# Which engine makes the rounded weight copies of the first MLP: ScalarE or GpSimd

## The chip, the core and the metric

The program runs on one core of a Trainium2 chip. The metric is the device time of one execution in microseconds. Four engines compute: TensorE (PE; its weight loads are shown as PEld), VectorE (DVE), ScalarE (ACT) and GpSimd (POOL). SyncE (SP) issues the DMA transfers.

## The reference

Windowed causal attention on 4 batches, 8 heads, 576 positions of dimension 64, and then two MLPs on the 2304 tokens of width 512, one behind the other:

```python
scores = scale * np.matmul(q, k.transpose(0, 1, 3, 2)) + slope[h] * -np.abs(rel)   # masked to 0 <= rel < 128
x = softmax(scores) @ v                                   # then tokens x 512
h = x @ w_in;   g = np.where(h >= 1, h, np.where(h <= -1, 0, (h + 1) ** 2 / 4));   x = g @ w_out     # 512 -> 2048 -> 512
h = x @ w_in2;  g = h * np.clip(h + 3.0, 0.0, 6.0) / 6.0;                          out = g @ w_out2
```

The MLP weights come as 64-bit floats.

## The kernel before

Matrix products run in a rounded 32-bit format (F32R). To keep accuracy every operand is held in two parts: a rounded copy, "hi", and the remainder, "lo" = x - hi. Each product is three matmuls (lo by hi, hi by lo, hi by hi). `split_hi(engine, hi, x)` writes the rounded copy and `split_lo` the remainder.

The weights of an MLP are converted on the chip, in 16 tiles f = 0 to 15 of 128 rows, each with 128 hidden columns of w_in and the matching 128 rows of w_out (2 x 512 numbers for each partition). SP loads the raw words into `raw`. `conv_tick` advances the conversion by one step: it issues the second and third part for tile f-1 and then the first part for tile f.

- `conv1`: ScalarE takes the magnitude of the high words (L194, into `m`); for the first MLP GpSimd makes the sign in place (L197, on every second word of `raw`); ScalarE rescales the low words (L198).
- `conv2`: VectorE shifts and joins (L205) and adds the low part (L212), both in `m`.
- `conv3`: the rounded copy of `m` goes to `hl[:, 0]` (the tile `w`, "wa" in the trace for the first MLP), on ScalarE (line L152, inside `split_hi`); VectorE makes the remainder (L159, inside `split_lo`).

`Weights("a", ..., True)` is the first MLP with `sign_pool` on; `Weights("b", ..., False)` the second MLP, which does without GpSimd.

The tokens of the first MLP go in blocks: three of 256 tokens, then four of 384. Attention for the first tokens runs alone with the first tiles' conversion; then blocks 0 and 1 take the hidden tiles 0 to 7, then both take tiles 8 to 15, while attention for later blocks is spread between (`run_block`, `spread`). For each tile f of a block TensorE does 12 matmuls into `h` (L659); VectorE, ScalarE and VectorE make the activation (L688, L689, L690), ScalarE copies its rounded part g (L152), GpSimd its remainder (L159); two tiles later (LAG = 2) 12 matmuls add it to `acc` (L701).

Attention in these stretches is: matmuls for scores (L411), row minimum on VectorE (L441), exponential on ScalarE (L445), transposes on TensorE (L469, L470), a copy to SBUF on ScalarE (L152, `tt`), matmuls with the values (L506), division on VectorE (L518 to L520), transpose (L531), and the split of x (ScalarE L152, VectorE L159).

SP's queue runs in the order written. On the other engines a planner of the framework orders the instructions up to the second MLP: it goes by the order in which the code traces them, and by when its own costs say that each is ready. Each engine then takes its instructions strictly in that order.

Of the kernel before, what the change touches and what calls it, by code (L numbers as in the profile page):

```python
# [40 lines left out]
def tile_window_attention_two_mlps(  # L41
# [108 lines left out]
    def split_hi(eng, hi, x):  # L150
        if eng == "act":
            nc.scalar.copy(hi, x)  # L152
        elif eng == "pool":
            nc.gpsimd.tensor_scalar(out=hi, in0=x, scalar1=1.0, scalar2=1.0, op0=ALU.mult, op1=ALU.mult)
        else:
            engines[eng].tensor_copy(hi, x)

    def split_lo(eng, lo, x, hi):
        engines[eng].tensor_tensor(out=lo, in0=x, in1=hi.bitcast(F32), op=ALU.subtract)  # L159
# [3 lines left out]
    class Weights:  # L163
# [50 lines left out]
        def conv3(self, f):  # L214
            del self.raw[f]
            m = self.m.pop(f)
            hl = wpool.tile([P, 2, 2, PIECE], F32R, tag=f"w{f}", name=f"w{self.nm}{f}")
            split_hi("act", hl[:, 0], m)
            split_lo("dve", hl[:, 1], m, hl[:, 0])
            self.hl[f] = hl  # L220

# [1119 lines left out]
```

## Time and profile before

| | |
|---|---|
| median of 3 runs | 948.38 us (946.82 to 948.67) |
| profiled execution | 947.39 us, span 945.7 us |
| TensorE busy | 929.6 us, 98% of the span |
| VectorE busy | 661.1 us, 70% |
| ScalarE busy | 534.0 us, 56% |
| GpSimd busy | 305.9 us, 32%, all of it before about 490 us |

TensorE's share is an average over stretches with different limits. What a change on another engine is worth has to be read from the stretch in which it acts: whether TensorE is idle there, and for whom it waits.

### The profile page before, as it was taken

The numbers are of one execution on the slowest core, as the hardware profiler recorded it, in microseconds if no ns is written. First come the engines' busy times: TensorE is split into PE (matmuls) and PEld (weight loads), VectorE is DVE, ScalarE is ACT, GpSimd is POOL, SyncE is SP. The second block draws the span as 40 slices with busy tenths as digits, with TensorE's granted clock in tenths as the row PEclk, the third lists the DMA queues.
The fourth block names the chain that finished last, engine by engine and source line by source line (L and its number), as shares of the span: only waits on it lengthen the run. The fifth ranks groups of instructions, "written<-read, shape, count | busy, mean of one in ns | idle before, by whom it ended". The sixth has DMA issues, their size and how long they took to land.

```text
span 945.7 us, 17240 instructions
## 1 busy us (share of the span) xinstructions
PE 929.6 (98%) x5683; PEld 875.8 (93%) x5683; DVE 661.1 (70%) x1750; ACT 534.0 (56%) x1349; POOL 305.9 (32%) x575
## 2 busy tenths in 40 slices
PE   8899999999999999999999999999999999999998
PEld 6799999999999999999999999999999898888987
DVE  5998975786677676767645999958557777644443
ACT  6998854676667566666634886535333334423233
POOL 3343854787668676767710000000000000000000
PEclk9999999999999999999999999999999999999999
DMA  9758332222212212222007861004264644544441
GB/s 263 233 168 262 112 99 88 68 81 72 73 54 82 72 52 62 80 84 56 7 34 249 304 235 59 1 23 167 79 211 166 236 170 147 170 124 114 122 113 67
DMA packets 95337, 114.90 MB, mean 122 GB/s; under 512 B 8848, under 2 KB 73616, under 8 KB 95248
## 3 DMA queue, kind: packets, MB, share of 16 engines
q1 hardware_dynamic: 95248, 113.80, 38.4%
q8 instruction: 45, 0.74, 0.3%
q14 instruction: 44, 0.36, 0.1%
HBM read 88.60 MB, written 25.17 MB: 120 GB/s over the span
## 4 chain that ended last, share of the span: by engine, by line
PE 86%; DVE 6%; DMA 3%; ACT 2%; issue 2%; POOL 0%; SPq 0%; ACTq 0%; POOLq 0%; DVEq 0%
PE h L659 25%; PE acc L760 21%; PE acc L701 17%; PE y L1242 7%; PE x L1242 5%; PE s L411 4%; PE r L554 3%; PE t L470 2%; PE r L506 1%; DMA rawa<-w_in 1%; DMA x2r<-x2d 1%; DVE r L688 1%; DMA kw<-kT 1%; DVE x L159 1%; DVE r L690 1%
## 5 line engine op out<-in xcount | busy, mean ns | idle before, releaser
L659 PE MATMUL h<-x,wa 128*128 128x384 f32 (+1 forms) x1344 | 231.0, 317 | 1.2 <-DVE r L690 0.8
L701 PE MATMUL acc<-g,wa 128*128 128x384 f32 (+1 forms) x1344 | 227.4, 315 | 0.4 <-POOL g L159 0.4
L760 PE MATMUL acc<-wb,g 128*128 128x512 f32 x861 | 222.2, 393 | 0.0
L659 PEld LDWEIGHTS h<-x,wa 128*128 128x128 f32 x1344 | 206.6, 189 | 4.4 <-DVE r L690 3.2
L701 PEld LDWEIGHTS acc<-g,wa 128*128 128x128 f32 x1344 | 206.2, 189 | 0.7 <-POOL g L159 0.6
L760 PEld LDWEIGHTS acc<-wb,g 128*128 128x128 f32 x861 | 159.4, 188 | 24.9
L152 ACT CAST g<-r 128x384 fp32r<-128x384 f32 (+1 forms) x208 | 101.3, 487 | 70.9 <-DVE r L1189 37.6
L159 POOL TENSOR_TENSOR g<-r,g 128x256 fp32r<-128x256 f32 (+1 forms) x96 | 92.9, 968 | 67.4 <-ACT g L152 54.3
L689 ACT ACTIVATE r<-r 128x384 f32<-128x384 f32 (+1 forms) x112 | 53.3, 478 | 82.9 <-DVE r L688 82.6
L159 DVE TENSOR_TENSOR g<-r,g 128x384 fp32r<-128x384 f32 x112 | 62.3, 557 | 41.9 <-ACT g L152 41.7
L688 DVE TENSOR_SCALAR r<-h 128x384 f32<-128x384 f32 (+1 forms) x112 | 55.4, 495 | 47.3 <-PE h L659 40.5
L488 POOL TENSOR_SCALAR_AFFINE_SELECT tt<-dist 128x256 fp32r<-128x256 f32 (+1 forms) x176 | 76.8, 457 | 14.1 <-DVE dist L483 13.9
L690 DVE TENSOR_TENSOR r<-h,r 128x384 f32<-128x384 f32 (+1 forms) x112 | 55.7, 499 | 29.7 <-ACT r L689 27.9
L659 PE MATMUL h<-x,wb 128*128 128x384 f32 x384 | 72.6, 336 | 0.0
L659 PEld LDWEIGHTS h<-x,wb 128*128 128x128 f32 x384 | 68.2, 188 | 2.6
L445 ACT ACTIVATE p<-p,sm 128x128 f32<-128x128 f32 (+2 forms) x134 | 56.9, 426 | 21.9 <-DVE sm L441 21.6
L1187 ACT ACTIVATE r<-u 128x384 f32<-128x384 f32 x32 | 16.8, 525 | 56.2 <-DVE u L1251 56.2
L554 PEld LDWEIGHTS r<-tt,vs 128*128 128x128 f32 x304 | 44.7, 189 | 3.5 <-issue 1.3
L393 POOL TENSOR_TENSOR qs<-qr,qs 128x256 fp32r<-128x256 f32 (+2 forms) x64 | 39.3, 616 | 25.0 <-ACT qs L390 13.3
L554 PE MATMUL r<-tt,vs 128*128 128x128 f32 (+3 forms) x304 | 44.3, 262 | 1.7 <-POOL tt L488 0.9
L391 DVE SCALAR_TENSOR_TENSOR kl<-kr,kh 128x256 fp32r<-128x256 f32 (+3 forms) x64 | 39.2, 613 | 0.0
L470 PE MATMUL t<-ident,p 128*128 128x128 f32 x134 | 38.4, 288 | 0.5 <-ACT tt L152 0.5
(161 smaller groups left out, 1554.3 us busy)
## 6 DMA issues: line engine op xcount, KB each, us to landing
w<-wd SPq DMA_DIRECT2D x88, 256.0 KB, 2.7
rawa<-w_in SPq DMA_DIRECT2D x16, 512.0 KB, 5.2
rawa<-w_out SPq DMA_DIRECT2D x16, 512.0 KB, 5.6
rawb<-w_in SPq DMA_DIRECT2D x16, 512.0 KB, 3.8
rawb<-w_out SPq DMA_DIRECT2D x16, 512.0 KB, 4.7
wd<-sum SPq DMA_DIRECT2D x32, 256.0 KB, 2.1
wd<-wb SPq DMA_DIRECT2D x24, 256.0 KB, 2.8
out<-o SPq DMA_DIRECT2D x17, 256.0 KB, 2.3
```

The source lines that it names most:

```text
L152: nc.scalar.copy(hi, x)
L159: engines[eng].tensor_tensor(out=lo, in0=x, in1=hi.bitcast(F32), op=ALU.subtract)
L445: nc.scalar.activation(out=pt[:, :nk], in_=pt[:, :nk], func=AF.Exp, bias=sm[:, 0:1], scale=-1.0, accum_out=None if u.whole else sm[:, 1:2])
L470: nc.tensor.transpose(ps[:, 1, :], pt[:, P:] if u.whole and has_prev else pt[:, :P], ident)
L488: nc.gpsimd.affine_select(out=u.tt[:, :, s0 + s, :m], in_=both, compare_op=ALU.is_ge, fill=0.0, base=-1 + s, pattern=[[0, 2], [sign, m]], ...
L554: nc.tensor.matmul(u.r[:, qo:qo + nq], u.vs[:, j, c, :, :].rearrange("p a d -> p (a d)"), u.tt[:, part].rearrange("p s q -> p (s q)")[:, s ...
L659: nc.tensor.matmul(ps[:, :n], self.W.w_in(a, c, f), self.x_chunk(x, b, c, n), start=(k == 0), stop=(k == 3 * KC - 1))
L688: nc.vector.tensor_scalar(out=r[:, :n], in0=ps[:, :n], scalar1=-1.0, scalar2=1.0, op0=ALU.max, op1=ALU.min)
L690: self.larger = nc.vector.tensor_tensor(out=r[:, :n], in0=ps[:, :n], in1=r[:, :n], op=ALU.max)
L701: nc.tensor.matmul(acc[i][:, o * n:(o + 1) * n], self.W.w_out(a, f)[:, e * P:(e + 1) * P], g[:, b, :n], start=(first and k == 0 and o == 0 ...
L760: nc.tensor.matmul(acc[t][:, :DM], g[:, b, tg * P:(tg + 1) * P], self.W.w_out(a, f), start=(first and k == 0), stop=(last and k == 2))
L1242: nc.tensor.matmul(ps[:, :N2], w[:, a, c * P:(c + 1) * P], self.x.operand(k, c, b), start=(start and n == 0), stop=(n == 5), skip_group_ch ...
```

## The change

The third part of the conversion asks for its rounded copy on GpSimd when `sign_pool` is on, that is for the 16 tiles of the first MLP. On GpSimd `split_hi` is a multiplication by 1.0 twice (`tensor_scalar`, L154), with the rounded format as its output. Block sizes and all else stay as they are.

```diff
             hl = wpool.tile([P, 2, 2, PIECE], F32R, tag=f"w{f}", name=f"w{self.nm}{f}")
-            split_hi("act", hl[:, 0], m)
+            split_hi("pool" if self.sign_pool else "act", hl[:, 0], m)
             split_lo("dve", hl[:, 1], m, hl[:, 0])
```

## Rows read from the trace of the kernel before

**Rows 1.** Stretches: window, us; PE, PEld, DVE, ACT, POOL busy; clock, DMA share, GB/s.

```profile
...
20.00:60.00 40.00, 35.08 (x252) 31.27 (x252) 36.76 (x86) 37.21 (x72) 13.29 (x12) 1.00 0.66 201
60.00:100.00 40.00, 39.96 (x336) 39.41 (x335) 35.13 (x99) 36.61 (x80) 18.85 (x29) 1.00 0.79 253
100.00:126.00 26.00, 25.57 (x215) 25.30 (x215) 25.86 (x50) 20.59 (x48) 19.01 (x17) 1.00 0.29 87
126.00:490.00 364.00, 360.72 (x2484) 354.31 (x2483) 250.10 (x935) 226.71 (x754) 248.61 (x496) 1.00 0.22 64
```

**Rows 2.** Waits of TensorE's weight loads, 20 to 60: us, times, longest.

```profile
...
PEld s L411 <- DVE sm L441: 3.1, 3, 1.4
PEld r L506 <- ACT tt L152: 1.3, 2, 0.8
...
PEld acc L701 <- POOL g L159: 0.6, 1, 0.6
```

**Rows 3.** Groups by form on GpSimd and ScalarE: busy us, mean ns, idle before.

```profile
...
L197 POOL TENSOR_SCALAR rawa<-rawa 128x1024 f32<-128x1024 f32 x16 | 22.5, 1407 | 40.8 <-ACT ma L194 31.3 <-DMA qw<-qT 9.5
...
L152 ACT CAST wa<-ma 128x1024 fp32r<-128x1024 f32 x16 | 16.7, 1044 | 2.9 <-DVE ma L212 2.8
```

**Rows 4.** ScalarE on the tile wa alone, by stretches (columns as in rows 1).

```profile
...
20.00:60.00 40.00, 6.28 (x6) 1.00 0.66 201
60.00:100.00 40.00, 6.25 (x6) 1.00 0.79 253
100.00:126.00 26.00, 4.18 (x4) 1.00 0.29 87
```

**Rows 5.** ScalarE in order of time: start, us.

```profile
...
21.17 1.03 ACT L152 CAST wa<-ma 128x1024 fp32r<-128x1024 f32 x1
...
22.41 0.34 ACT L152 COPY tt<-t 128x256 f32<-128x256 f32 x1
...
38.50 1.05 ACT L152 CAST wa<-ma 128x1024 fp32r<-128x1024 f32 x1
39.45 0.40 ACT L152 CAST g<-r 128x256 fp32r<-128x256 f32 x1
```

**Rows 6.** TensorE's weight loads in order of time.

```profile
...
22.81 0.52 PEld L506 LDWEIGHTS r<-vr,tt 128*128 128x128 f32 x4 [0.81 <-ACT tt L152]
...
41.44 0.53 PEld L701 LDWEIGHTS acc<-g,wa 128*128 128x128 f32 x4 [0.59 <-POOL g L159]
...
114.96 1.50 PEld L701 LDWEIGHTS acc<-g,wa 128*128 128x128 f32 x12
```

**Rows 7.** GpSimd in order of time.

```profile
...
33.04 1.17 POOL L197 TENSOR_SCALAR rawa<-rawa 128x1024 f32<-128x1024 f32 x1 [4.84 <-ACT ma L194]
38.13 1.28 POOL L197 TENSOR_SCALAR rawa<-rawa 128x1024 f32<-128x1024 f32 x1 [3.92 <-ACT ma L194]
...
49.98 1.15 POOL L197 TENSOR_SCALAR rawa<-rawa 128x1024 f32<-128x1024 f32 x1 [3.48 <-ACT ma L194]
...
104.59 2.11 POOL L197 TENSOR_SCALAR rawa<-rawa 128x1024 f32<-128x1024 f32 x1
...
113.13 1.71 POOL L159 TENSOR_TENSOR g<-r,g 128x256 fp32r<-128x256 f32 x1
```

**Rows 8.** VectorE in order of time.

```profile
...
31.50 1.20 DVE L212 CUSTOM_DVE_ANT_0 ma<-rawa,ma 128x2048 uint16<-128x2048 uint16 x1
...
34.25 1.23 DVE L205 SCALAR_TENSOR_TENSOR ma<-ma,rawa 128x1024 uint32<-128x1024 uint32 x1 [0.88 <-POOL rawa L197]
...
37.19 1.22 DVE L212 CUSTOM_DVE_ANT_0 ma<-rawa,ma 128x2048 uint16<-128x2048 uint16 x1
...
50.00 2.20 DVE L212 CUSTOM_DVE_ANT_0 ma<-rawa,ma 128x2048 uint16<-128x2048 uint16 x1
```

**Rows 9.** VectorE on the tile ma alone (L205, L212, L159), by stretches.

```profile
...
60.00:100.00 40.00, 20.18 (x18) 1.00 0.79 253
100.00:126.00 26.00, 17.97 (x12) 1.00 0.29 87
```

## The prediction

> **What bounds the kernel now.** I read the stretches of the span first [rows 1]. From 60 to 490 us TensorE is hardly ever idle: 0.04 us of 40 between 60 and 100, 0.43 of 26 between 100 and 126, 3.3 of 364 between 126 and 490. The granted clock is 1.00 throughout, the upper level of 2.4 GHz. So the kernel's length is TensorE's work plus the gaps in front of it, and a change off TensorE counts only where it opens or closes such gaps. Of the stretches in which casts are moved, the one with gaps is 20 to 60: TensorE busy 35.08 of 40, 4.92 us idle, with VectorE at 36.76 (92%) and ScalarE at 37.21 (93%). GpSimd has 13.29 us there, a third. In 100 to 126 VectorE is full (25.86 of 26), ScalarE at 79%, GpSimd at 73%.
>
> Next, who TensorE waits for in 20 to 60 [rows 2]. Its weight loads wait 3.1 us for VectorE's row minimum of the scores (L441), 1.3 us for ScalarE's copies of the transposed scores (L152) and 0.6 us for GpSimd's remainder of g (L159). VectorE is the larger wait, ScalarE the busier engine. The change unloads ScalarE, and adds to an engine that gets in VectorE's way (below).
>
> Then the moved instruction: 16 casts of 128x1024, 1044 ns each on ScalarE [rows 3], six in 20 to 60, six in 60 to 100, four in 100 to 126 [rows 4]. None is left at 126; the second MLP's weights keep ScalarE.
>
> **The change part by part.**
>
> *Taken from ScalarE:* 16 x 1.044 = 16.7 us; in 20 to 60 it is 6.28 of 37.21 us [rows 1, 4], which leaves 30.9 of 40. What TensorE gets of it I look for at its waits. Twice a cast stands right in front of what TensorE waits for. At 21.17 the cast runs for 1.03 us, and the copy of the transposed scores behind it starts at 22.41 [rows 5]; the weight load that needs it had waited 0.81 us [rows 6]. At 38.50 a cast of 1.05 us delays the rounded copy of g to 39.45 [rows 5], GpSimd's remainder follows it, and the load at 41.44 had waited 0.59 us [rows 6]. Gain on the path: 0.81 + 0.59 = 1.40 us. The other waits in that stretch have VectorE or another ScalarE step in front, so nothing is surely gained there. Bound: all of the 4.92 us, unlikely since 3.1 us are VectorE's; I take 1.40.
>
> *Added to GpSimd:* 16 multiplications by one, 128x1024 to rounded f32. The trace of before has no such write with this shape. The nearest row is the sign step L197, the same operation and element count on every second word: mean 1407 ns over 16 [rows 3], 1.15 us at 49.98 and 2.11 at 104.59 [rows 7]. Bounds 1.15 and 2.1 us each, 18 to 34 us in all. In 20 to 60 that is 6 x 1.2 = 7 us on 13.29, room enough. In 100 to 126 it is 4 x 1.15 to 4 x 2.1 = 4.6 to 8.4 us on 19.01, which makes 23.6 to 27.4 of 26: GpSimd fills up there.
>
> *What it is queued among.* GpSimd takes its instructions in order, and in one tick of the conversion it has the sign step of tile f to do just when the copy of tile f-1 becomes ready. VectorE's add (L212) ends at 32.70 and 38.41 [rows 8], where the copy could start; the sign steps start at 33.04 and 38.13 [rows 7]. So one waits for the other, for 0.8 to 1.1 us. If the copy goes first, the sign step is about 0.85 us late, and VectorE's next step of that tile, which already had 0.88 us of idle in front of it at 34.25 for this very reason [rows 8], comes later with everything behind it. If the sign step goes first, the copy ends some 1.0 us later than on ScalarE at the second of the two. Price on TensorE: 0 to 0.85 each, 0 to 1.7 for the pair. I take one of them, 0.85, as VectorE has idle time to give back in that stretch (3.2 us of 40). What else waits behind GpSimd is the remainder of g, made two hidden tiles ahead of its use; the slack there is small only in 100 to 126.
>
> *VectorE and GpSimd meet.* At 49.98 a sign step starts on GpSimd and runs 1.15 us; VectorE's add, begun at 50.00, takes 2.20 us where its like at 31.50 took 1.20 [rows 7, 8]. The add lost 1.0 us, about what was left of GpSimd's step. VectorE's three steps of a tile (L205, L212, L159) all have two operands in SBUF, and they are most of its work in 100 to 126: 17.97 of 25.86 us [rows 1, 9]. Their mean is 20.18/18 = 1.12 us in 60 to 100, where GpSimd is busy 47%, and 17.97/12 = 1.50 in 100 to 126, where it is busy 73%: 12 x 0.38 = 4.5 us more, by 17 GpSimd instructions of together 19.01 us, 0.24 us for each us. A copy of 1.15 to 2.1 us then costs VectorE 0.27 to 0.5 us, and 1.0 us at the worst seen. The Trainium skill, "SBUF — State Buffer", section "Who interferes with whom", says that a VectorE instruction with two SBUF inputs and a GpSimd instruction that reads SBUF exclude each other, and the later one blocks entirely; the trace agrees (2.20 against 1.20 us). By that page alone a copy could block up to its whole 1.15 us, 18 us over the 16; the rows give 0.27 to 0.5.
>
> *By stretch.* In 60 to 100 TensorE is full and VectorE has 4.9 us idle [rows 1]; six copies at 0.4 us are 2.4 us, hidden: 0. It would cost those 2.4 us if VectorE were full. In 100 to 126 there is no cover. VectorE is full, and the remainder of g that ends at 113.13 + 1.71 = 114.84 [rows 7] is read by TensorE at 114.96 [rows 6]: 0.12 us of slack. Four copies at 0.4 us are 1.6 us, less 0.12: **+1.5 us**. Bounds: 0 (the planner puts the conversions behind the activation, which tiles 12 to 15 can afford: by the order of the blocks they are used after tiles 8 to 11) and 4 x 1.0 - 0.12 = 3.9. After 126 no moved instruction is left: 0. The planner that orders the engines will order them anew, and what that shifts I cannot read from any row.
>
> *The sum:* -1.40 + 0.85 + 1.5 = +0.95 us. On the profiled execution that is 947.39 + 0.95 = 948.3 (its span is 945.7, with 1.7 around it). That execution lay 0.99 us under the median of the runs, 948.38, which is what will be compared, so I predict 948.38 + 0.95 = **949.3 us**, +0.1%. A measurement of this kernel tells about 0.2%, 1.9 us, from no change.
>
> **The rivals.**
>
> *Slower: GpSimd and VectorE in each other's way at 100 to 126.* For it: VectorE has no idle time there, GpSimd would be 91 to 105% busy, and the slack of g is down to 0.12 us. Against it: the tiles converted there are used last, and the stretch after 126 has room on both. Each copy costs its worst, 3.9 us, and both tick conflicts fall on TensorE, 1.7, less the 1.40 gained: +4.2, **952.6 us**. It decides from about 0.65 us lost per copy in that stretch (4 x 0.65 - 0.12 - 0.55 = 1.93).
>
> *Faster: ScalarE was the tighter of the two in 20 to 60.* With 6.28 us less to do its short steps in the attention chain (exponentials, transposed copies) start at once, and TensorE gets back half of what it still waits there, (4.92 - 1.40)/2 = 1.8, besides 1.40: -3.2, with conflicts and late loss near 0.2: **945.4 us**. For it: ScalarE is at 93% there, and GpSimd, two thirds idle, could start each copy as soon as the add ends. Against it: the largest wait is VectorE's, whose work does not shrink.
>
> *No change at all, hidden:* the stretch 20 to 60 gives nothing and 100 to 126 takes nothing, since the planner finds room: 948.4. It shares the side of my forecast.
>
> **How the numbers follow.** My sum and the hidden case, both within 0.2%: 0.43. The slower rival and what lies between it and the sum above 950.3: 0.36. The faster rival: 0.21. The range runs from the faster rival, 945.4, to both upper bounds of the losses with only the first gain of 0.81, 948.38 + 3.9 + 1.7 - 0.8 = 953.2. Within it the likeliest case itself reaches from 947.0 to 950.3.
>
> **What would show it.** ScalarE some 16.7 us less busy, GpSimd 18 to 34 more, the copies 1.15 to 2.1 us each. In 20 to 60 TensorE's idle time near 4.4 us (3 or less: the faster rival). In 100 to 126 TensorE's idle time near 1.9 us, VectorE's two-operand steps above 1.5 us on average, weight loads waiting for the remainder of g or for VectorE's maximum (L690); 4 us or more: the slower rival. I am wrong if the gaps after 126 change by more than 1 us, for then the new order, not the copies, made the difference, or if the copy is dearer than 2.1 us undisturbed.

## The result, and the profile after

The changed kernel takes 957.96 us (median of 4 runs, 957.14 to 959.34), the kernel before 947.62 beside it: ratio 1.011, interval 1.0092 to 1.0128, so 10.3 us slower. The forecast was 949.3, and the result lies outside its range. The profiled execution of the changed kernel took 959.34 us, span 957.6, against 945.7. It is the slowest of the four, with a mean clock of 0.996; the other three ran at 1.000 and took 957.14 to 958.20.

The stretches come first again (columns as in [rows 1]; the last one goes on to 500).

```profile
20.00:60.00 40.00, 34.68 (x241) 30.71 (x242) 36.53 (x84) 30.63 (x62) 20.65 (x19) 0.96 0.71 205
60.00:100.00 40.00, 38.24 (x318) 37.45 (x316) 36.46 (x89) 30.13 (x69) 23.84 (x31) 1.00 0.76 250
100.00:126.00 26.00, 21.85 (x172) 20.57 (x171) 22.10 (x44) 16.24 (x37) 20.53 (x19) 1.00 0.19 54
126.00:140.00 14.00, 12.13 (x91) 12.16 (x92) 11.79 (x25) 6.02 (x19) 6.57 (x8) 0.88 0.20 63
...
140.00:500.00 360.00, 356.80 (x2453) 350.37 (x2452) 247.51 (x926) 224.32 (x749) 247.39 (x494) 1.00 0.22 65
```

The kernel before, where it has not been shown yet:

```profile
126.00:140.00 14.00, 14.00 (x121) 14.00 (x120) 8.64 (x35) 7.36 (x22) 7.29 (x13) 1.00 0.34 100
```

TensorE's idle time is now 5.32 us in 20 to 60 (before 4.92), 1.76 in 60 to 100 (0.04), 4.15 in 100 to 126 (0.43) and 1.87 in 126 to 140, where the kernel before has 14.00 busy of 14. From 140 to 500 TensorE is busy 356.8 of 360, before 356.7. So the loss is made before 140. Over the whole span TensorE is idle for 24.3 us (957.6 - 933.3) against 16.1: 8.2 of the 11.9 us between the two spans. The other 3.7 us are busy time, and the clock column says where: 0.96 and 0.88 in two stretches, against 1.00 all through before. That part belongs to this execution. The three without it are only 1.1 to 2.2 us shorter, so the lower clock explains little of the 10.3 us between the medians.

VectorE's three steps of a tile and GpSimd's copy, grouped by form (busy us, mean ns, idle before):

```profile
L159 DVE TENSOR_TENSOR wa<-ma,wa 128x1024 fp32r<-128x1024 f32 x16 | 26.3, 1642 | 6.2 <-POOL wa L154 6.2
...
L205 DVE SCALAR_TENSOR_TENSOR ma<-ma,rawa 128x1024 uint32<-128x1024 uint32 x16 | 23.6, 1475 | 0.7 <-POOL rawa L197 0.6
...
L212 DVE CUSTOM_DVE_ANT_0 ma<-rawa,ma 128x2048 uint16<-128x2048 uint16 x16 | 21.4, 1336 | 0.0
...
L154 POOL TENSOR_SCALAR wa<-ma 128x1024 fp32r<-128x1024 f32 x16 | 18.7, 1172 | 10.9 <-DMA kw_kl<-kT 3.8 <-DVE ma L212 3.6 <-DMA kw<-kT 3.5
```

The same three steps in the kernel before:

```profile
L212 DVE CUSTOM_DVE_ANT_0 ma<-rawa,ma 128x2048 uint16<-128x2048 uint16 x16 | 21.7, 1355 | 0.0
L205 DVE SCALAR_TENSOR_TENSOR ma<-ma,rawa 128x1024 uint32<-128x1024 uint32 x16 | 21.3, 1334 | 1.5 <-POOL rawa L197 1.4
L159 DVE TENSOR_TENSOR wa<-ma,wa 128x1024 fp32r<-128x1024 f32 x16 | 21.0, 1311 | 0.4 <-ACT p L445 0.2
```

The three steps together took 71.3 us; before they took 64.0. The remainder (L159) grew by 5.3 us, the joining step (L205) by 2.3, the add (L212) not at all. The copies cost 1172 ns on average. And the remainder waited 6.2 us for its copy; before it waited hardly at all. The waits of 20 to 140 us (us, times, longest), against [rows 2]:

```profile
DVE wa L159 <- POOL wa L154: 6.2, 7, 2.8
...
PEld s L411 <- DVE sm L441: 3.9, 4, 1.5
...
PEld r L506 <- issue: 2.5, 1, 2.5
...
PEld h L659 <- DVE r L690: 2.5, 1, 2.5
...
PEld h L659 <- DVE wa L159: 2.1, 3, 1.5
...
PEld acc L701 <- POOL g L159: 1.9, 2, 1.4
```

One of VectorE's waits, followed to TensorE, in order of time from 115 to 128:

```profile
115.67 1.21 DVE L212 CUSTOM_DVE_ANT_0 ma<-rawa,ma 128x2048 uint16<-128x2048 uint16 x1
115.70 1.79 POOL L393 TENSOR_TENSOR qs<-qr,qs 128x256 fp32r<-128x256 f32 x1
...
117.45 2.08 POOL L159 TENSOR_TENSOR vs<-vr,vs 128x192 fp32r<-128x192 f32 x2
...
119.50 1.13 POOL L197 TENSOR_SCALAR rawa<-rawa 128x1024 f32<-128x1024 f32 x1
...
120.59 1.05 POOL L154 TENSOR_SCALAR wa<-ma 128x1024 fp32r<-128x1024 f32 x1
...
121.60 0.73 POOL L159 TENSOR_TENSOR g<-r,g 128x256 fp32r<-128x256 f32 x1
121.67 1.73 DVE L159 TENSOR_TENSOR wa<-ma,wa 128x1024 fp32r<-128x1024 f32 x1 [2.77 <-POOL wa L154]
...
122.38 1.37 PEld L701 LDWEIGHTS acc<-g,wa 128*128 128x128 f32 x11 [1.41 <-POOL g L159]
...
123.33 0.41 DVE L690 TENSOR_TENSOR r<-h,r 128x256 f32<-128x256 f32 x1
...
127.84 0.30 PEld L506 LDWEIGHTS r<-vr,tt 128*128 128x128 f32 x2 [2.55 <-issue]
```

The copy could start at 116.88, when the add (L212) ends. In front of it GpSimd had three remainders for attention, then the sign step of the next tile, and it ran at 120.59, 3.7 us late. VectorE stood at the head of its queue for 2.77 us. Behind it stood the activation (L690, 123.33), which ScalarE, GpSimd and, two hidden tiles later, TensorE's matmuls into `acc` need. The profile puts the gap of 2.55 us before 127.84 down to no engine ("issue"), so that this wait leads to it is not shown. On GpSimd the remainder of g stood behind the copy, and TensorE's weight load waited 1.41 us for it.

The rows hold a second thing. The remainder at 121.67 starts 0.07 us behind GpSimd's next instruction and takes 1.73 us, where undisturbed ones take some 1.2. Six of the 16 remainders start so, right behind the instruction that follows the copy on GpSimd, and take 1.73 to 2.15 us: the end of the copy lets both engines go on at once. Another such place, with the sign step as that next instruction:

```profile
40.06 1.17 POOL L197 TENSOR_SCALAR rawa<-rawa 128x1024 f32<-128x1024 f32 x1
40.14 2.14 DVE L159 TENSOR_TENSOR wa<-ma,wa 128x1024 fp32r<-128x1024 f32 x1 [0.16 <-POOL wa L154]
```

The gain that I had counted did not come. Where the cast of tile 0 had stood on ScalarE [rows 5], the rescaling step L198 moved up, and TensorE's wait behind it was 0.91 us, before 0.81 [rows 6]:

```profile
20.93 1.15 ACT L198 ACTIVATE rawa<-rawa 128x1024 int32<-128x1024 uint32 x1
...
22.26 0.34 ACT L152 COPY tt<-t 128x256 f32<-128x256 f32 x1
...
22.66 0.52 PEld L506 LDWEIGHTS r<-vr,tt 128*128 128x128 f32 x4 [0.91 <-ACT tt L152]
```

### The profile page after: what moved, and what is told of

Read it like the earlier page. It is cut to its first block, busy times and chain, and to the rows that moved or that the text cites. A ratio compares the mean times of both kernels' runs of the same rounds, so it can differ in the third digit from the quotient of the medians.

```text
span 957.6 us, 17251 instructions
## 1 busy us (share of the span) xinstructions
PE 933.3 (97%) x5683; PEld 878.2 (92%) x5683; DVE 668.1 (70%) x1750; ACT 521.2 (54%) x1333; POOL 325.1 (34%) x591
## 4 chain that ended last, share of the span: by engine, by line
PE 87%; DVE 5%; ACT 2%; DMA 2%; POOL 1%; issue 1%; SPq 0%; ACTq 0%; POOLq 0%; DVEq 0%
PE h L659 25%; PE acc L760 21%; PE acc L701 18%; PE y L1242 7%; PE x L1242 5%; PE s L411 4%; PE r L554 3%; PE t L470 2%; PE r L506 1%; DMA rawa<-w_out 1%; DVE wa L159 1%; DMA kw_kl<-kT 1%; DMA x2r<-x2d 1%; DVE r L688 1%; DVE r L690 1%
## 5 line engine op out<-in xcount | busy, mean ns | idle before, releaser
L159 POOL TENSOR_TENSOR g<-r,g 128x256 fp32r<-128x256 f32 (+1 forms) x96 | 95.3, 993 | 61.5 <-ACT g L152 50.3
L159 DVE TENSOR_TENSOR g<-r,g 128x384 fp32r<-128x384 f32 x112 | 62.3, 556 | 41.7 <-ACT g L152 41.4
L690 DVE TENSOR_TENSOR r<-h,r 128x384 f32<-128x384 f32 (+1 forms) x112 | 55.6, 497 | 28.7 <-ACT r L689 26.7
L1242 PE MATMUL y<-wb,w 128*128 128x384 f32 x192 | 38.7, 336 | 0.0
```

Of the source, the lines that this page charges most:

```text
L690: self.larger = nc.vector.tensor_tensor(out=r[:, :n], in0=ps[:, :n], in1=r[:, :n], op=ALU.max)
L1242: nc.tensor.matmul(ps[:, :N2], w[:, a, c * P:(c + 1) * P], self.x.operand(k, c, b), start=(start and n == 0), stop=(n == 5), skip_group_ch ...
```

## The experiments

Three causes are possible: GpSimd and VectorE exclude each other (the copies lengthen VectorE's steps); VectorE waits for copies that stand late in GpSimd's queue; and the planner's new order costs by itself. (Below, two orders are compared by the fewest instructions of an engine's queue that stand elsewhere; by that count 153 of TensorE's 5683 weight loads and 65 of VectorE's 1750 instructions stand elsewhere in the changed kernel than in the kernel before.) Each run below is compared with runs of the kernel before on the same chip (their medians were 946.9 to 947.4). "Steps" is the sum of VectorE's three steps of the 16 tiles, 64.0 us before and 71.3 after; the 61.6 and 68.6 us of one expectation are the part of them between 20 and 140 us.

**Half of the copies.** `split_hi("pool" if self.sign_pool and f < KF // 2 else "act", ...)`, and the same with `f >= KF // 2`.

> GpSimd makes the copies of tiles 0 to 7, ScalarE those of tiles 8 to 15. Queue theory (VectorE's remainder, next in its queue, waits for a copy that stands behind attention work and sign steps in GpSimd's queue; this hurts where GpSimd is full, at 100 to 126 us): tiles 12 to 15 are back on ScalarE, so most of the 10.3 us is gone, 948 to 952, and TensorE's idle time in 100 to 140 is under 2 us. Exclusion theory (each copy simply blocks VectorE's two-operand steps): half the copies, about half the loss, 951 to 954. Order theory (the planner's new order, not the copies, costs the time): cannot say, anything from 946 to 958.

> GpSimd makes the copies of tiles 8 to 15, ScalarE those of tiles 0 to 7. Queue theory: most of the loss stays, 954 to 958, with VectorE waiting some 3 to 6 us for copies between 75 and 126 us. Exclusion theory: about half the loss, 951 to 954. Order theory: anything from 946 to 958.

Measured: tiles 0 to 7 gave 952.04, +4.8 (1.0051, 1.0036 to 1.0066), tiles 8 to 15 gave 950.87, +3.6 (1.0039, 1.0025 to 1.0053). Steps 67.7 and 66.5; VectorE waited 0.9 and 2.1 us for copies. So the loss doesn't sit in 100 to 126 alone, where I had put all of it. But the two halves are not alike, for the planner treats them differently. With the late copies moved the queues are nearly those of the kernel before (27 weight loads and 17 instructions on VectorE elsewhere), and TensorE's added idle time lies in 100 to 126 (3.29 us, before 0.43): that is the copies, almost without a new order. With the early copies moved the queues are nearly those of the changed kernel (11 and 13 elsewhere), and TensorE is idle for 2.42 us in 100 to 126 although the last moved copy is made at 72 us. That points to the new order. The late copies also show that the engines hold each other up both ways; here VectorE came first, and the copy took 1.99 us instead of 1.05:

```profile
97.73 1.22 DVE L205 SCALAR_TENSOR_TENSOR ma<-ma,rawa 128x1024 uint32<-128x1024 uint32 x1
97.86 1.99 POOL L154 TENSOR_SCALAR wa<-ma 128x1024 fp32r<-128x1024 f32 x1
```

**The remainder one tick later.** All copies on GpSimd, but VectorE's remainder of tile f-1 is written down a tick later (or just before the tile is first used), so that its copy has long been made.

```diff
+                self.remainder(n - 2)     # split_lo of the tile before; conv3 only makes the copy
```

> GpSimd makes all 16 copies as in the changed kernel, but VectorE's remainder is traced one step of the conversion later, or just before the tile is first used. Same instructions, nothing left out. Queue theory: VectorE's wait for the copies falls from 6.2 us to under 1.5, and the time to 947 to 952. Exclusion theory: the lengthening of VectorE's steps on the tile (68.6 against 61.6 us) stays, and the time stays at 955 to 959.

Measured: 956.96, +9.7 (1.010, 1.0081 to 1.012). VectorE's wait for copies was gone and the steps were down to 67.8, and the time hardly moved. In its place VectorE waited 2.0 us for sign steps and 2.1 for remainders of g, and TensorE 2.5 us for a remainder of g. That speaks against the theory that the queue wait by itself is the cause. It doesn't refute it alone, since the planner's order is another one here too (some 130 weight loads elsewhere than in the changed kernel).

**The load without the place.** All copies stay on ScalarE. GpSimd gets 16 more multiplications by one of `m`, in place, behind the remainder, so that nobody on VectorE waits for them. Two controls: the same as a memset, which writes as much but reads nothing, and on 8 words of 1024.

```diff
             split_lo("dve", hl[:, 1], m, hl[:, 0])
+            if self.sign_pool:
+                nc.gpsimd.tensor_scalar(out=m, in0=m, scalar1=1.0, scalar2=1.0, op0=ALU.mult, op1=ALU.mult)
```

> ScalarE makes all copies as before; GpSimd gets 16 additional multiplications by one, in place on the tile m after VectorE's remainder has read it, which nothing waits for but the next use of that buffer. It is GpSimd's load of the change without the wait. Queue theory: at most 3 us slower than before, 947 to 951. Exclusion theory: as slow as the changed kernel or slower, 955 to 960, since VectorE's steps meet as many GpSimd steps and ScalarE is not unloaded.

> As e4, but GpSimd's 16 additional instructions are memsets of the tile m instead of multiplications: as many words written at the same places of every queue, and nothing read. Every engine's instructions stand in the same order as in e4. Exclusion theory (a GpSimd instruction that reads SBUF and VectorE's two-operand steps hold each other up): most of e4's 8 us is gone, 947 to 951, and VectorE's steps on the tile m are as short as before, 61 to 63 us. Queue theory (GpSimd simply has more to do in its own order, and the remainder of g and the sign steps behind it come late): as slow as e4, 953 to 957. Order theory: as slow as e4, since the order is the same.

> As e4, but the additional multiplications by one are on 8 of the 1024 words of each row: the same dependences, hardly any load. Exclusion theory and queue theory: back to 947 to 949. Order theory: stays at 953 to 957, as the new order is nearly that of e4.

Measured: the multiplication 955.52, +8.3 (1.0091, 1.0057 to 1.0124, four runs from 952.07 to 960.22); the memset 949.61, +2.7 (1.0028, 1.0014 to 1.0043, 10 runs); 8 words 949.74, +2.8 (1.0025, 1.0014 to 1.0036, 10 runs). The first two have the same instructions in the same order on every engine, but for that one operation, and nearly the order of the kernel before (3 weight loads and 8 instructions on VectorE elsewhere). By form, the multiplication and then the memset:

```profile
L212 DVE CUSTOM_DVE_ANT_0 ma<-rawa,ma 128x2048 uint16<-128x2048 uint16 x16 | 23.1, 1444 | 0.0
...
L221 POOL TENSOR_SCALAR ma<-ma 128x1024 f32<-128x1024 f32 x16 | 18.7, 1171 | 15.2 <-DVE wa L159 8.3 <-DMA kw_kh<-kT 3.4 <-ACT tt L152 2.9
```

```profile
L212 DVE CUSTOM_DVE_ANT_0 ma<-rawa,ma 128x2048 uint16<-128x2048 uint16 x16 | 19.7, 1229 | 0.0
...
L221 POOL MEMSET ma<- 128x1024 f32 x16 | 15.3, 953 | 14.6 <-DVE wa L159 8.4 <-ACT tt L152 2.9 <-DMA qw<-qT 2.8
```

VectorE's add takes 1444 ns beside the multiplications and 1229 beside the memsets. The steps add up to 67.1 and 61.7 (62.0 with 8 words). So 15.3 us of writing on GpSimd cost VectorE nothing, while 18.7 us of an operation that also reads lengthened its steps by 5.4 us and the kernel by 5.6 (8.3 - 2.7, each against the kernel before on its own chip; by the two intervals some 2.5 to 9.4). That the memset is a little shorter than the multiplication can't be the reason: 16 instructions of 8 words, 5.2 us in all, cost the kernel as much as 15.3 us of memsets. So GpSimd's time alone costs nothing that shows here, and what the operation reads does: that is the exclusion, on the path. The profiled executions can't tell where all of it goes, since the multiplications' one had TensorE busy for 3.5 us longer, with a clock of 0.96 in 20 to 60. The remaining 2.8 us of the controls have another cause, which the traces don't show: the executions profiled took 948.05 and 948.07, some 1.6 us less than the medians.

**The place without more exclusion.** Copy on GpSimd, sign step on ScalarE as a scaling by zero (signs left out).

```diff
-                nc.gpsimd.tensor_scalar(out=sign, in0=sign, scalar1=0.0, ...)
+                nc.scalar.activation(out=sign, in_=sign, func=AF.Copy, scale=0.0)
```

> GpSimd makes the rounded copies, and ScalarE the sign step that GpSimd had (a copy scaled by zero, which need not keep the sign, so the weights can come out without it). Each engine has about the load of before, only the copy now passes GpSimd. Exclusion theory: GpSimd reads SBUF no more than before, 946 to 950. Queue theory: VectorE's remainder still waits for a copy behind other work, 951 to 955.

Measured: 952.99, +6.1 (1.0065, 1.004 to 1.0089). The steps were 62.4, no longer than before, and VectorE waited 7.0 us for copies (read from the slowest of the four executions, 956.5). So with no added exclusion there is still a loss of 6 us; but the order is new here too.

**The copies on VectorE.** `split_hi("dve" ...)`: nobody waits for GpSimd.

> VectorE makes the rounded copies of the first MLP itself; GpSimd has its work of before, ScalarE is unloaded as in the change. It shows what the unloading of ScalarE is worth against VectorE's time. Exclusion theory: VectorE loses the copy's own time, 16 x 0.6 to 1.1 us, without GpSimd's interference: 950 to 956. If ScalarE's load mattered much, 945 to 949.

Measured: 958.68, +11.8 (1.0113, 1.009 to 1.0135). A copy costs 955 ns there, 15.3 us in all, and VectorE is busy 38.9 of 40 us between 100 and 140. The order is new here as well (some 160 weight loads elsewhere).

**The changed kernel with less reading, in its own order.** The copies as memsets of the same tile to zero, and the sign steps as memsets. Both kernels keep the changed kernel's order on every engine (the queues are the same, instruction by instruction).

```diff
-            split_hi("pool" if self.sign_pool else "act", hl[:, 0], m)
+                nc.gpsimd.memset(hl[:, 0].bitcast(F32), 0.0)
...
-                nc.gpsimd.tensor_scalar(out=sign, in0=sign, scalar1=0.0, ...)
+                nc.gpsimd.memset(sign, 0.0)
```

> The changed kernel with GpSimd's 16 copies replaced by memsets of the same tile to zero: they stand in the same place of the chain (after VectorE's add, before its remainder), take about as long, and read nothing. The rounded part of the weights is left out, so the whole weight goes into the remainder. Exclusion theory: the steps on the tile m shrink from 71 to about 64 us in all, and the time falls from 958 by 4 to 6 us, to 952 to 954. Place theory (what costs is that VectorE waits for GpSimd in its queue, as in e5): VectorE still waits 4 to 7 us and the time stays at 955 to 958. If both are at work: 951 to 955, with the waits left and the steps short.

> The changed kernel with GpSimd's 16 sign steps replaced by memsets, which read nothing; the signs of the first MLP's weights are left out. All engines' instructions stand in the order of the changed kernel. Exclusion theory: GpSimd now reads SBUF for the conversion as often as before the change, so some 4 to 6 us come back, 952 to 954. Order theory (the new order of all engines costs the time): 957 to 958 as the changed kernel.

Measured: without the copies' reading 952.17, +4.8 (1.0052, 1.0039 to 1.0065), 5.6 us less than the changed kernel's loss (10.34 - 4.77); without the signs' reading 954.06, +6.7 (1.0068, 1.0053 to 1.0082), 3.7 less (10.34 - 6.66), both give or take some 2 us. Steps 67.8 and 65.1 instead of 71.3; VectorE's waits for the copies 4.1 and 4.8 instead of 6.2. So what GpSimd reads costs 4 to 6 us in the changed kernel's own order as well. Part of that comes as shorter waits, since each instruction on GpSimd is shorter too.

The 67.8 are a miss: I had expected about 64. The remainder is what stayed long without the copies' reading, and what became shorter without the signs':

```profile
L159 DVE TENSOR_TENSOR wa<-ma,wa 128x1024 fp32r<-128x1024 f32 x16 | 25.7, 1607 | 4.1 <-POOL wa L219 4.1
```

```profile
L159 DVE TENSOR_TENSOR wa<-ma,wa 128x1024 fp32r<-128x1024 f32 x16 | 22.1, 1380 | 4.8 <-POOL wa L154 4.8
```

In the place of 40.06 above, with a memset for the sign step, the remainder is not lengthened:

```profile
38.58 1.06 POOL L197 MEMSET rawa<- 128x1024 f32 x1
38.67 1.23 DVE L159 TENSOR_TENSOR wa<-ma,wa 128x1024 fp32r<-128x1024 f32 x1 [0.16 <-POOL wa L154]
```

So most of what the steps grew by is not the copy's own reading. The copy on GpSimd makes the remainder begin together with the instruction that follows the copy there, and that one's reading lengthens it. The joining step, 20.5 us without the copies' reading against 23.6 with it, is the one that the copies themselves lengthen.

**One copy.** Only tile 0's is on GpSimd (`f == 0`).

> Only tile 0's copy on GpSimd, the one that stood in front of TensorE's first wait of 0.81 us, in a stretch where GpSimd and VectorE are both free for it. If the gain at that place is real: 0.3 to 0.8 us faster than before. If the new order decides: anything within 3 us of before on either side.

Measured: 951.7, +4.3 (1.0047, 1.0032 to 1.0063, 6 runs). One copy of about 1 us is too short to cost that by its own time. VectorE waits for no copy of GpSimd's in this kernel. But the queues differ from those of the kernel before: some 130 weight loads and 70 instructions on VectorE stand elsewhere.

**The order alone.** Every instruction on its old engine; in `conv_tick` the first part for tile f is written down ahead of the rest of tile f-1.

```diff
+            if n < KF and self.sign_pool:
+                self.conv1(n)
             if n > 0:
                 self.conv2(n - 1)
                 self.conv3(n - 1)
-            if n < KF:
+            if n < KF and not self.sign_pool:
                 self.conv1(n)
```

> The kernel before, with every instruction on its old engine (all sixteen copies on ScalarE, nothing new on GpSimd); only the place in the program changes at which the conversion of the first MLP's weights is written down, one block's copy ahead of the previous block's remaining steps, so that the planner orders the work anew. Order theory (a new order alone is worth some microseconds, as the run with a single moved copy, +4.3 us, suggests): 2 to 5 us off the kernel before, most likely above it, with VectorE's two-operand steps on the weights as long as before (about 64 us in all) and the idle time of TensorE between 20 and 140 us of the span changed. Rival (the single moved copy costs through GpSimd and its queue): within 1 us of the kernel before.

Measured: 952.17 against 947.28, +4.9 (1.0058, 1.0044 to 1.0072; by the ratio 5.5 us, which is the figure that the expectations below quote). The steps are 63.0 us, no longer than before. The stretches:

```profile
20.00:60.00 40.00, 34.43 (x228) 31.32 (x229) 33.74 (x80) 34.41 (x64) 11.86 (x12) 0.91 0.68 199
60.00:100.00 40.00, 39.32 (x327) 38.51 (x326) 36.46 (x99) 37.07 (x81) 16.63 (x27) 1.00 0.77 248
100.00:126.00 26.00, 24.81 (x210) 24.61 (x210) 23.30 (x49) 21.86 (x48) 21.60 (x19) 1.00 0.28 86
126.00:140.00 14.00, 14.00 (x122) 14.00 (x121) 10.57 (x35) 8.33 (x24) 5.39 (x10) 1.00 0.25 73
```

And ScalarE and TensorE in order of time (line numbers behind the edit are larger by 2):

```profile
21.10 1.15 ACT L198 ACTIVATE rawa<-rawa 128x1024 int32<-128x1024 uint32 x1
...
22.84 0.52 PEld L508 LDWEIGHTS r<-vr,tt 128*128 128x128 f32 x4 [0.89 <-ACT tt L152]
...
23.81 1.05 ACT L152 CAST wa<-ma 128x1024 fp32r<-128x1024 f32 x1
...
40.72 0.75 PEld L661 LDWEIGHTS h<-x,wa 128*128 128x128 f32 x4 [2.38 <-DVE r L692]
```

At 21 us L198 has gone in front of the cast, the same exchange as in the changed kernel, and TensorE waits as long behind it (0.89 us). Later comes a wait of 2.38 us for VectorE's activation. The kernel with one moved copy has it too (2.4), the changed kernel 2.48 at 39.28, and the kernel before has none like it [rows 2]. So a new order can cost some 5 us with no instruction moved to another engine. It is not the changed kernel's order: 130 weight loads stand elsewhere than there, and 121 elsewhere than in the kernel before.

**Copies and order, crossed.** The first part written down between the second and the third, with the copies on ScalarE and on GpSimd, and the text order of the run above with the copies on GpSimd.

> The kernel before, every instruction on its old engine; a second order alone: the conversion's first part for tile f is written down between the second and the third part for tile f-1. Order theory (the order of before is a good one, and most others are some microseconds worse, as the first one tried, +5.5 us): +2 to +6 us. Rival (the first one tried was bad by its own place): within 1.5 us of the kernel before.

> All sixteen copies on GpSimd as in the changed kernel, with the first part for tile f written down between the second and the third part for tile f-1, so that the copy is planned behind the next sign step. Theory of order and place (the two engines' mutual exclusion stays at 4 to 6 us, order and queue waits take the rest): 6 to 14 us over the kernel before, in any case 3 us or more over the same order with the copies on ScalarE. Rival (the changed kernel's loss is mostly its unlucky order): within 2 us of the same order with the copies on ScalarE.

> All sixteen copies on GpSimd, with the first part for tile f written down ahead of all that is left of tile f-1; the same text order with the copies on ScalarE took +5.5 us. Theory of order and place: 4 to 6 us of exclusion over that, +9 to +12 over the kernel before. Rival (mostly an unlucky order): +4 to +7.

Measured against 947.13: 952.35, +5.2 (1.0051, 1.0033 to 1.0069); 958.21, +11.1 (1.0113, 1.0089 to 1.0138); 958.93, +11.8 (1.0117, 1.0097 to 1.0137). Laid beside each other, the engines' queues show that these are no new orders: the first has the order of the run above, and the other two have that of the changed kernel, instruction by instruction. They tell nothing of other orders, then, but repeat two measurements: the order alone +4.9 and +5.2, the changed kernel +10.3, +11.1 and +11.8. They also show that with the copies on GpSimd the planner puts the first part ahead whichever way the text has it. Under the same text, the copies on GpSimd cost 5.9 and 6.9 us more than on ScalarE (11.1 - 5.2, 11.8 - 4.9); the two orders that are compared so are not the same, as said above.

No kernel tried was faster than the kernel before.

## Why the prediction was wrong

**The order: the step that failed.** "The planner that orders the engines will order them anew, and what that shifts I cannot read from any row": I entered it with nothing. The runs showed in its place that a new order alone is worth some 5 us: +4.9 and +5.2 with no instruction on another engine, +4.3 with one copy moved. What the changed kernel's own order costs is not isolated. With the copies' reading taken out, in exactly that order, +4.8 us were left; in them are the order, the waits for GpSimd's queue and what the memsets cost. So order and place together have about half of the loss, which is an estimate, the difference of two medians; how it divides between the two stays open. My own mark for a new order, gaps after 126 that change by more than 1 us, looked in the wrong place: that gap did grow by 1.87 us in the changed kernel, but the kernel with the order alone has no gap there at all (14.00 of 14). Its cost is spread from 20 to 126, with 0.65, 0.64 and 0.76 us more of idle time in the three stretches, and the clock (last section).

**The gain of 1.40: wrong, by the same step.** I took the cast away and left everything else in its place. The planner had another long step to put there (L198), and the wait stayed: 0.91 against 0.81. At the second place it was 0.50 us at 42.92 against 0.59.

**The exclusion: right in kind, too small in reach.** I took 0.4 us per copy, 6.4 for 16, and let 1.5 of them reach TensorE. The price was, if anything, high: 16 multiplications lengthened VectorE's steps by 5.4 us, 0.34 each, and the copies' own reading in the changed kernel by 3.5 (71.3 - 67.8), 0.22 each. (Its working was loose: the 4.5 us of 100 to 126 lie above the mean of 60 to 100, where GpSimd was at work too, but I divided them by all of GpSimd's 19.01 us.) The term that was mis-sized is what reaches TensorE: 5.6 us for the multiplications in nearly the old order and 5.6 for the copies' reading in the new one (with the shorter waits in it), where I had +1.5. I had let only the four copies of 100 to 126 count, called the six of 60 to 100 hidden, since VectorE had 4.9 us idle there, and charged those of 20 to 60 with the queue conflict only. Between the multiplications' execution and the memsets', TensorE's idle time differs by 1.62 us in 20 to 60, 0.55 in 60 to 100 and 0.56 in 100 to 126, so the stretch that I had left out has the most of it; in the changed kernel that of 60 to 100 rose from 0.04 to 1.76. And I did not see that the copy would set VectorE's remainder against the next instruction on GpSimd.

The rule quoted in the prediction (the Trainium skill, "SBUF — State Buffer", section "Who interferes with whom") also says that a GpSimd instruction that only writes does not meet VectorE's second operand. The runs agree: 61.7 us of steps beside memsets, 67.1 beside multiplications. Single instructions show nearly the whole block, on whichever engine came second: 2.14 us for a remainder, 1.99 for a copy. The 18 us that I worked out from that page as the most it could come to did not occur.

**The queue: seen, and read from the wrong side.** I asked what happens when a copy and a sign step are ready together (0.85), and what else waits behind GpSimd. I did not ask what stands in front of the copy from attention, nor that VectorE's remainder comes to the head of its queue and holds all behind it: 6.2 us of waiting, the longest 2.77. What it costs by itself stays open. Taking it away, under yet another order, moved the waits to the sign steps and to g (956.96).

**The slower rival.** It had the mechanism of 100 to 126, and TensorE's idle time there, 4.15 us, passed its mark of 4. But it gave 952.6 for all 16 copies. The late eight alone took 950.87, within its reach and in its stretch. The early eight cost +4.8 with nearly the changed kernel's order, and no case of mine had a loss there.

**What held.** The copy's price, 1172 ns on average, lies in the bounds of 1.15 to 2.1 us; undisturbed it was 1.04 to 1.05 (115 to 128 above), just under the lower one. Beyond 140 us nothing changed. ScalarE's busy time fell by 12.8 us, not by the 16.7 that left it: busy time counts a stretch once in which two instructions overlap, as the cast of 38.50 does with the next instruction, at 39.45 [rows 5], and no other group of ScalarE's grew by more than 0.3 us.

## What to carry to other kernels

Where a planner orders the queues, a change of engine is two changes. What a new order can cost is tried alone: keep every instruction where it is and alter the text order, before or beside the real change. Then compare the queues, for the order that comes out need not be that of the real change; here it was not. When work goes to an engine that is one third busy, read four things there: what stands in its queue in front of the moved instruction and what right behind it, which engine stops at the head of its own queue until it is done, and whether its operand reads meet the reads of the engine that paces the stretch. A control in the same order, such as a memset in the place of a copy, separates the reading from the rest in one pair of runs.

## What was unexpected of the hardware

The granted clock fell behind two gaps of TensorE. Windows of the changed kernel behind the gap that ended at 39.28 (2.48 us) and around the one that ended at 127.84 (2.55 us):

```profile
40.00:45.00 5.00, 4.79 (x27) 4.37 (x26) 3.90 (x9) 2.85 (x9) 3.59 (x4) 0.66 0.53 174
...
125.00:130.00 5.00, 2.63 (x20) 2.45 (x19) 5.00 (x14) 2.42 (x8) 4.72 (x5) 0.92 0.33 95
130.00:135.00 5.00, 5.00 (x35) 5.00 (x35) 3.52 (x6) 2.11 (x6) 0.79 (x2) 0.74 0.31 107
```

And its weight loads around the second, in order of time:

```profile
117.16 1.51 PEld L701 LDWEIGHTS acc<-g,wa 128*128 128x128 f32 x12
...
128.50 2.21 PEld L701 LDWEIGHTS acc<-g,wa 128*128 128x128 f32 x12
```

Twelve loads took 2.21 us behind the gap and 1.51 some 11 us earlier. The upper level is 2.4 GHz and the lower one 1.2. Not every such gap does it: the kernel with tiles 0 to 7 on GpSimd had a weight load that waited 2.45 us at 39.76, with the clock at 1.00 in 35 to 40 and in 40 to 45. The kernel with the order alone shows 0.91 over 20 to 60, and its mean clock was 0.994 to 0.996 in all five runs, against 0.999 to 1.0 of the kernel before. Of the 4.3 us between those two spans, 2.6 us are longer TensorE busy time (932.2 against 929.6). A gap thus cost a second time, at the clock. But it does not belong to the order: the same queues, run again, had mean clocks of 0.994 to 1.000, and the run at 1.000 took 950.97, still 3.8 us over the kernel before. What decides which gap does so, the runs do not show.
